# A decay scan that silences its neighbour rows through a byte table of its own, in a linear-attention and expert kernel

## The chip, the cores and the metric

One Trainium2 chip, one core. The metric is device time in microseconds (us) for one execution. PE is the matrix engine (PEld its weight loads), DVE the vector engine, ACT the scalar engine, POOL the GpSimd engine, SP the engine whose queue issues most DMAs. SBUF is the working memory and PSUM the accumulator memory that PE writes.

## The reference

Two parts follow each other. The first is a linear attention with a decaying state, over 4 batches, 8 heads, 768 tokens and a head size of 48:

```
for t in range(S):
    cur = einsum('bhd,bhe->bhde', u * k[t], v[t])
    y[:, :, t] = einsum('bhd,bhde->bhe', r[t], state + cur)
    state = w[t][..., None] * state + einsum('bhd,bhe->bhde', k[t], v[t])
```

The second takes `y` as 3072 tokens of 384 numbers. A token with `x @ w_skip > 0` goes to the best of 8 experts by `x @ w_gate`; its row becomes `x + gate * (relu(x @ w1[e]) @ w2[e])`. The other rows stay as they are.

## The kernel before

**Attention.** The tokens are cut into 24 chunks of 128 (6 for each batch). A chunk's decays `w`, reads `r` and keys `k` lie in one SBUF tile `wrk` (three of them take turns): partitions hold head halves and channels, the free axis holds 4 head pairs of 130 columns for `w` (128 decays and two zeros, with a head column in front), and 4 times 128 for `r` and `k`. Only partitions 16 to 111 are the chunk's own rows. The load brings all 128, so that the 32 outer ones are rows of neighbouring chunks; `rowsk` is a column that holds 1 on the chunk's own partitions and 0 on the others.

Two scans on DVE turn the decays into products. `prep_scan` (L274) runs backwards, `state = max(state * w, table)`, where the byte table `ones_at`, kept in the PSUM tile `pss`, holds a 1 at the end of each head pair, so that the products start anew there. The result `q` is each position's product to the end of the chunk. `prep_keys` takes the reciprocal of the whole product (L290) and puts it at the four head columns of `w`. `prep_reads` (L299) scans forwards over these heads and decays and gives `rh`, the factor of the reads. For all chunks but the first, the reciprocal goes to `hd`, four words of `pss`, and a multiplication by `rowsk` (L292) carries it to the head columns: neighbours' heads become 0, and so do their rows of `rh`.

POOL multiplies: `rk = r*k` (L283), `kq = k*q` (L294), `rp = r*rh` (L304). PE then works through a fixed order in each round: `update` (L359), `outputs` (L378 and L382 into `psY`), `scores` of the next chunk (L326 into `psA`), a transpose (L316), `bonus_sums` (L345 into `psY`) and `rows_out` (L394). Between scores and outputs, DVE masks the scores (L332, twice) and scales the bonus in place in `psY` (L349); L378 adds to `psY` and so waits for L349. ACT evicts `psY` (L387, `xT`), and L345 of the next chunk waits for that.

**Router.** After each 6 chunks a generator `router` is dripped into the following rounds: small DVE operations (L412 to L464, most with results in `pss`), a few matmuls into `pss` (ranks, L435 to L440; places, L511), and the rows `hot` of 256 columns, which ACT makes, but for some by DVE in `one_hot` (L470). For the last two chunks of the third group, `one_hot` compares with `iotap`, a copy of the counting row in `pss`; for the last group with `iota` in SBUF.

**Experts.** From about 156 us on PE runs the 8 experts with weights split in two parts.

In attention the order on each engine is the order in which the code is written: in round `s` the calls are `update(s)`, `carry(s)`, `prep_scan(s+2)`, router pieces, `outputs(s)`, `prep_keys(s+2)`, `prep_reads(s+2)`, `evict(s)`, `scores(s+1)`, `mask(s+1)`, `bonus(s+1)`. Waits between engines are placed by a framework that follows tiles: a write to one part of `pss` is ordered behind other engines' work on `pss`, too.

Of the kernel before, what the change touches and what calls it, by code (L numbers as in the profile page):

```python
# [8 lines left out]
F32 = mybir.dt.float32  # L9
BF16 = mybir.dt.bfloat16  # L10
F32R = mybir.dt.float32r
I32 = mybir.dt.int32
U32 = mybir.dt.uint32
U8 = mybir.dt.uint8
AF = mybir.ActivationFunctionType
ALU = mybir.AluOpType
# [5 lines left out]
P = 128  # L22
# [5 lines left out]
NP = H // 2  # L28
# [3 lines left out]
CW = P + 2  # L32
# [24 lines left out]
def rwkv_moe_kernel(ctx, tc, wrk, wrk0, vN, uP, wgs, wgp, w12, cst, out):  # L57
    nc = tc.nc
# [63 lines left out]
    with tc.tile_pool(name="att", bufs=2) as att, \  # L122
# [52 lines left out]
        rowsk = keep.tile([P, 1], F32, name="rowsk")  # L175
        ident = c_sb[:, C_ID:C_ID + P]
        tri = c_sb[:, C_TRI:C_TRI + P]
        iota = keep.tile([P, 2 * P], BF16, name="iota")
# [26 lines left out]
        def scratch(words):  # L205
            at = [next(at_) for _ in range(words)][0]
            return pss[:, at:at + words]

        ones_w = scratch(NP * CW // 4 + 1)
        ones_at = ones_w.bitcast(U8)  # L210
        hd = scratch(NP).rearrange("p (a o) -> p a o", o=1)
        iotaw = scratch(P)
        iotap = iotaw.bitcast(BF16)
        small3 = {nm: scratch(NC * w).rearrange("p (c e) -> p c e", c=NC)
                  for nm, w in (("lg", E + 1), ("dl", E), ("km", 1), ("sm", 1))}

        def clear_w(eng, i):
            eng.memset(wrk_sb[i][:, :R_OFF], 1.0)
# [4 lines left out]
        def setup():  # L223
            clear_w(nc.gpsimd, 0)
            nc.gpsimd.memset(vt_sb[0], 0.0)
            clear_rk(nc.vector, 0)
            load_chunk(0)
            nc.vector.memset(warm, 0.0)
            nc.gpsimd.memset(vt_sb[1], 0.0)
            load_chunk(1)  # L230
            load_v(0)
            nc.vector.memset(pss, 0.0)
            ints = ones_w.bitcast(U32)
            for a in range(NP):
                at = (a + 1) * CW - 1
                nc.vector.memset(ints[:, at // 4:at // 4 + 1], 1 << 8 * (at % 4))
            nc.vector.tensor_reduce(rowsk, ident[:, KO:LO], axis=AX, op=ALU.add)
            nc.scalar.activation(junk0, warm[:, 0:1], AF.Exp)
            for z in psa:
                nc.scalar.copy(z.rearrange("p a j -> p (a j)"), warm)  # L240
            nc.gpsimd.memset(vt_sb[2], 0.0)
            nc.scalar.copy(ubk_sb, u_sb.rearrange("p (a o) -> p a o", o=1).to_broadcast([P, NP, D]))
            for g in range(2):
                nc.tensor.matmul(psy2[:, g].rearrange("p s j -> p (s j)"), warm[:, :P], warm,
                                 start=True, stop=True, skip_group_check=True)
            nc.tensor.matmul(psu.rearrange("p a j -> p (a j)"), warm[:, :P], warm[:, :NP * HP],
                             start=True, stop=True, skip_group_check=True)
# [38 lines left out]
        def prep_keys(i):  # L286
            wk = work[i]
            heads = wk["w"][:, 0:NP * CW].rearrange("p (a j) -> p a j", a=NP)
            at = heads[:, :, 0:1]
            nc.vector.reciprocal(hd if i > 0 else at, wk["q"][:, :, 0:1])  # L290
            if i > 0:
                nc.vector.tensor_scalar(at, hd, rowsk, None, op0=ALU.mult)  # L292
            kq = wk["kq"] = att.tile([P, NP, P], F32, tag="kq", name=f"kq{i}")
            nc.gpsimd.tensor_tensor(kq, wk["k"], wk["q"][:, :, 1:1 + P], op=ALU.mult)  # L294

        def prep_reads(i):
            wk = work[i]
            rh = wk["rh"] = att.tile([P, NP, CW], F32, tag="rh", name=f"rh{i}", bufs=2)
            nc.vector.tensor_tensor_scan(  # L299
                rh.rearrange("p a j -> p (a j)"), wk["w"][:, 0:NP * CW], ones_at[:, :NP * CW],  # L300
                1.0, op0=ALU.mult, op1=ALU.max)
            rp = wk["rp"] = att.tile([P, NP, P], F32, tag="rp", name=f"rp{i}", bufs=3)
            eng = nc.gpsimd if i > 0 else nc.vector
            eng.tensor_tensor(rp, wk["r"], rh[:, :, :P], op=ALU.mult)  # L304
# [101 lines left out]
        def router(i0, m):  # L406
# [17 lines left out]
                                           op0=ALU.is_gt, op1=ALU.mult)  # L424
# [38 lines left out]
            r1 = rall[:, i0:i0 + m]  # L463
# [3 lines left out]

            def one_hot(c):
                hot = att.tile([P, 2 * P], BF16, tag="hot", name=f"hot{i0}_{c}", bufs=NC)
                nc.vector.tensor_scalar(hot, iota if last else iotap, r1[:, c], None,  # L470
                                        op0=ALU.is_equal)
                hots[c] = hot

# [7 lines left out]
            last = i0 + m == n  # L481
# [104 lines left out]

        with tc.manual_schedule():
            setup()
            fill(FILL0)
            for s in range(-2, n + 1):  # L590
                on = lambda i: 0 <= i < n
                if s + 4 < n:
                    load_chunk(s + 4)
                if on(s + 3) and s + 3 >= 1:
                    load_v(s + 3)
                if s == -2:
                    to = wgp_sb.rearrange("p (s g) x -> p g s x", g=2)
                    nc.sync.dma_start(to[:, 0, :, :2 * D], wgp[:, :2, :2 * D])
                    for o in range(2):
                        nc.sync.dma_start(to[half(o), 1, :, :2 * D], wgp[half(1 - o), :2, :2 * D])  # L600
                        for g in range(2):
                            at = 2 * (g ^ o)
                            nc.sync.dma_start(to[half(o), g, :, 2 * D:],
                                              wgp[half(g), at:at + 2, 2 * D:])
                if s == 1:
                    nc.sync.dma_start(c_sb[:, C_IOTA:], cst[:, C_IOTA:])
                if s == LATE:
                    nc.sync.dma_start(wgs_sb, wgs)
                if on(s - 1):
                    store(s - 1)  # L610
                for i0, m in GROUPS:
                    if i0 + m == s:
                        pace[0] = 1 if i0 + m < LATE else 2
                        later.append(router(i0, m))
                        if i0 + m == LATE:
                            later.append(early())
                if on(s):
                    update(s)
                    carry(s)
                if on(s + 2):  # L620
                    prep_scan(s + 2)
                drip(pace[0])
                if on(s):
                    outputs(s)
                flush()
                if on(s + 2):
                    prep_keys(s + 2)
                    drip(pace[0])
                    if s != -1:
                        prep_reads(s + 2)  # L630
                if s == -2:
                    bonus_keys(0)
                    nc.gpsimd.memset(vt_sb[3], 0.0)
                    nc.gpsimd.memset(onesb, 1.0)
                    nc.gpsimd.memset(ohs, 0.0)
                    nc.gpsimd.memset(key, 0.5)
                if on(s):
                    evict(s)
                if on(s + 1):
                    scores(s + 1)  # L640
                    rows_of_keys(s + 1)
                    drip(2 * pace[0])
                    mask(s + 1, 0)
                    mask(s + 1, 1)
                    drip(pace[0])
                    bonus_sums(s + 1)
                    bonus(s + 1)
                if s == -1:
                    prep_reads(1)
                if on(s + 2):  # L650
                    prep_check(s + 2)
                for _ in range(min(2, len(marks))):
                    marks.popleft()()
                if s == n - 1:
                    early_tokens(0)
                if on(s):
                    rows_out(s)
                flush()
                if s in (1, 2, 3):
                    nc.scalar.copy(*((trib, tri), (identb, ident),  # L660
                                     (iota, c_sb[:, C_IOTA:C_IOTA + 2 * P]))[s - 1])
                if s == 4:
                    nc.scalar.copy(iotaw, iota.bitcast(F32))
                k = s + 1 - W_AT
                for eq, k0 in (((0, 1), 0), ((1, 0), 9), ((0, 0), 16), ((1, 1), 18)):
                    if k == k0:
                        gens[eq] = load_weights(*eq)
                    if k0 <= k < k0 + 3:
                        next(gens[eq])
                if 3 <= k < 9:  # L670
                    split_slice(0, 3 + k, nc.gpsimd)
                if 12 <= k < 18:
                    split_slice(1, k - 12, nc.gpsimd)
# [349 lines left out]
```

## Time and profile before

| | |
|---|---|
| time, median of 3 (lowest to highest) | 302.96 us (302.51 to 303.55) |
| the profiled execution's own time | 301.18 us |
| its span in the trace | 299.4 us |
| PE busy | 275.0 us (92%) |
| DVE busy | 223.8 us (75%) |
| ACT busy | 168.1 us (56%) |
| POOL busy | 138.6 us (46%) |

The span is from the first to the last instruction in the trace; 1.78 us of the profiled time lie outside it. Shares are means over attention (about 10 to 156 us) and experts (from there to the end), which have different limits. Times in rows are us from the span's start.

### The profile page before, as it was taken

How to read it: one execution, taken by the hardware profiler on the slowest of the kernel's cores; microseconds unless marked ns; L12 is line 12 of the kernel's file. 1: busy time of each engine (PE TensorE's matmuls, PEld its weight loads, DVE VectorE, ACT ScalarE, POOL GpSimd, SP SyncE). 2: the span in 40 equal slices, each digit the busy share in tenths (PEclk: the TensorE clock that was granted, in tenths of full speed). 3: DMA queues.
4: the chain of work that ended last, by engine and by line, in shares of the span. 5: the costliest groups of instructions: out<-in, count | busy, mean ns of one | idle time of the engine just before them, and what ended most of it. 6: DMA issues, size and time to landing. Idle time of an engine off the chain costs nothing.

```text
span 299.4 us, 8963 instructions
## 1 busy us (share of the span) xinstructions
PE 275.0 (92%) x3581; PEld 247.8 (83%) x3581; DVE 223.8 (75%) x434; ACT 168.1 (56%) x470; POOL 138.6 (46%) x136
## 2 busy tenths in 40 slices
PE   6697998998889979879999999999999999999993
PEld 2476877777767867768798999999999999999993
DVE  7869999898989988986373788784958859496320
ACT  3265645779565986587432485581837649183310
POOL 4867765969975689776115761402011020201101
PEclk9999999999999999999999999999999999999999
DMA  7979999996799968865604798866265663620001
GB/s 217 246 198 311 349 352 371 309 303 194 240 332 297 333 187 285 219 210 180 209 28 114 231 373 308 274 207 234 71 231 208 210 251 129 237 107 26 9 2 41
DMA packets 26548, 64.62 MB, mean 216 GB/s; under 512 B 4886, under 2 KB 15930, under 8 KB 26496
## 3 DMA queue, kind: packets, MB, share of 16 engines
q1 hardware_dynamic: 23904, 58.14, 59.4%
q0 software_dynamic: 2048, 5.48, 5.5%
q8 instruction: 30, 0.49, 0.7%
q10 hardware_dynamic: 544, 0.33, 0.6%
q14 instruction: 22, 0.18, 0.2%
HBM read 56.88 MB, written 7.86 MB: 216 GB/s over the span
## 4 chain that ended last, share of the span: by engine, by line
issue 32%; PE 12%; DVE 7%; DMA 7%; POOL 6%; ACT 5%; POOLq 1%; SPq 0%; DVEq 0%
POOL out L745 5%; DMA r<-w 4%; PE psY L378 2%; PE psH L115 2%; PE psA L326 2%; PE psX L394 2%; DMA vt<-wrk 2%; PE psY L382 1%; DMA xg<-out,idr 1%; PE psY L345 1%; DVE w2l L90 1%; DVE psY L349 1%; DVE asb L332 1%; ACT xT L387 1%; PE psT L316 1%
## 5 line engine op out<-in xcount | busy, mean ns | idle before, releaser
L745 POOL DMA_INDIRECT out<-fin,ids x16 | 16.9, 1058 | 101.1 <-DVE fin L840 93.3
L814 ACT ACTIVATE hh<-psH 128x256 fp32r<-128x256 f32 x60 | 23.1, 384 | 55.2 <-PE psH L809 52.1
L809 PE MATMUL psH<-xTh,w1l 128*128 128x256 f32 x168 | 47.5, 283 | 0.0
L808 PE MATMUL psH<-xTl,w1h 128*128 128x256 f32 x168 | 47.5, 283 | 0.0
L807 PE MATMUL psH<-xTh,w1h 128*128 128x256 f32 x168 | 47.5, 283 | 0.0
L831 PE MATMUL psO<-w2h,hh 128*128 128x384 f32 x120 | 40.9, 341 | 0.0
L833 PE MATMUL psO<-w2h,hl 128*128 128x384 f32 x120 | 40.2, 335 | 0.0
L832 PE MATMUL psO<-w2l,hh 128*128 128x384 f32 x120 | 40.1, 334 | 0.0
L819 DVE SCALAR_TENSOR_TENSOR hl<-psH,hh 128x256 fp32r<-128x256 f32 x60 | 25.2, 420 | 12.3 <-ACT hh L814 12.0
L378 PE MATMUL psY<-asb,v 128*48 128x128 f32 x384 | 26.5, 276 | 8.4 <-DVE psY L349 8.4
L304 POOL TENSOR_TENSOR rp<-wrk,rh 128x512 f32<-128x512 f32 x23 | 27.2, 1182 | 12.5 <-DVE rh L299 7.6
L283 POOL TENSOR_TENSOR rk<-wrk 128x512 f32<-128x512 f32 x24 | 31.3, 1304 | 3.6 <-DMA wrk<-wrk 3.6
L332 DVE TENSOR_TENSOR asb<-psA,c_sb 128x512 f32<-128x512 f32 x48 | 30.5, 677 | 3.0 <-PE psA L326 2.8
L274 DVE TENSOR_TENSOR_SCAN q<-wrk,pss 128x520 f32<-128x520 f32 x24 | 29.3, 1222 | 4.5 <-DMA wrk<-wrk 4.4
L294 POOL TENSOR_TENSOR kq<-wrk,q 128x512 f32<-128x512 f32 x24 | 28.3, 1180 | 8.6 <-DVE q L274 4.7
L809 PEld LDWEIGHTS psH<-xTh,w1l 128*128 128x128 f32 x168 | 32.2, 192 | 0.0
L808 PEld LDWEIGHTS psH<-xTl,w1h 128*128 128x128 f32 x168 | 32.2, 192 | 0.0
L807 PEld LDWEIGHTS psH<-xTh,w1h 128*128 128x128 f32 x168 | 32.2, 191 | 0.0
L299 DVE TENSOR_TENSOR_SCAN rh<-wrk,pss 128x520 f32<-128x520 f32 x24 | 29.7, 1236 | 1.7
L89 ACT CAST w2h<-r 128x512 fp32r<-128x512 f32 x48 | 27.9, 625 | 2.0 <-DMA r<-w 2.0
L90 DVE TENSOR_TENSOR w2l<-r,w2h 128x512 fp32r<-128x512 f32 x42 | 27.8, 687 | 1.5 <-ACT w2h L89 0.5
L378 PEld LDWEIGHTS psY<-asb,v 128*48 128x48 f32 x384 | 20.4, 123 | 10.0 <-DVE psY L349 9.8
(149 smaller groups left out, 594.3 us busy)
## 6 DMA issues: line engine op xcount, KB each, us to landing
r<-w SPq DMA_DIRECT2D x48, 512.0 KB, 5.3
wrk<-wrk SPq DMA_DIRECT2D x22, 772.5 KB, 5.8
v<-vN SPq DMA_DIRECT2D x24, 192.0 KB, 5.2
out<-x SPq DMA_DIRECT2D x24, 192.0 KB, 4.6
vt<-wrk SPq DMA_DIRECT2D x46, 96.0 KB, 5.3
wrk<-wrk SPq DMA_DIRECT2D x1, 579.4 KB, 4.8
wrk<-wrk SPq DMA_DIRECT2D x1, 384.0 KB, 4.4
out<-fin,ids POOLq DMA_INDIRECT x16, 3.9
```

The costliest lines, as they stand in the source:

```text
L90: (eng or nc.vector).tensor_tensor(dst_l, src, dst_h.bitcast(F32), op=ALU.subtract)
L283: nc.gpsimd.tensor_tensor(work[i]["rk"].rearrange("p a j -> p (a j)"), t[:, R_OFF:K_OFF], t[:, K_OFF:V_OFF], op=ALU.mult)
L299: nc.vector.tensor_tensor_scan(rh.rearrange("p a j -> p (a j)"), wk["w"][:, 0:NP * CW], ones_at[:, :NP * CW], 1.0, op0=ALU.mult, op1=ALU.max)
L332: nc.vector.tensor_tensor(s, psa[g], tri.rearrange("p (o j) -> p o j", o=1).to_broadcast([P, NP, P]), op=ALU.mult)
L378: nc.tensor.matmul(y_at(a, g), v[:, 2 * a + g], wk["asb"][g][:, a], start=False, stop=True, skip_group_check=True)
L745: sc = nc.gpsimd.indirect_dma_start(out=out, out_offset=bass.IndirectOffsetOnAxis(ap=ids[:, s % 2, s // 2:s // 2 + 1], axis=0), in_=o, in_ ...
L807: nc.tensor.matmul(ps, w1h[:, o:o + P], xTh[:, kc], start=(kc == 0), stop=False)
L808: nc.tensor.matmul(ps, w1h[:, o:o + P], xTl[:, kc], start=False, stop=False)
L809: nc.tensor.matmul(ps, w1l[:, o:o + P], xTh[:, kc], start=False, stop=(kc == KC - 1))
L831: nc.tensor.matmul(pso, h[j, fc][0], w2h[:, o], start=(fc == 0), stop=False)
L832: nc.tensor.matmul(pso, h[j, fc][0], w2l[:, o], start=False, stop=False)
L833: nc.tensor.matmul(pso, h[j, fc][1], w2h[:, o], start=False, stop=(fc == FC - 1))
```

## The change

The second scan gets a byte table `reads_at` of its own, made once in `setup` by multiplying `ones_at` (seen as 32-bit words) with `rowsk`, and its start value becomes the column `rowsk` in place of the number 1. On a neighbour's rows it starts with 0 and never finds a 1, so that they come out 0 whatever stands at the heads. The reciprocal then writes the head columns directly for every chunk, and the multiplication goes. `hd` and the copy `iotap` make room in `pss`; `one_hot` always reads `iota` in SBUF, and ACT's copy to `iotap` goes.

```diff
-        hd = scratch(NP).rearrange("p (a o) -> p a o", o=1)
-        iotaw = scratch(P)
-        iotap = iotaw.bitcast(BF16)
+        reads_w = scratch(NP * CW // 4 + 1)
+        reads_at = reads_w.bitcast(U8)
...
             nc.vector.tensor_reduce(rowsk, ident[:, KO:LO], axis=AX, op=ALU.add)
+            nc.vector.tensor_scalar(reads_w.bitcast(U32), ints, rowsk, None, op0=ALU.mult)
...
-            at = heads[:, :, 0:1]
-            nc.vector.reciprocal(hd if i > 0 else at, wk["q"][:, :, 0:1])
-            if i > 0:
-                nc.vector.tensor_scalar(at, hd, rowsk, None, op0=ALU.mult)
+            nc.vector.reciprocal(heads[:, :, 0:1], wk["q"][:, :, 0:1])
...
             nc.vector.tensor_tensor_scan(
-                rh.rearrange("p a j -> p (a j)"), wk["w"][:, 0:NP * CW], ones_at[:, :NP * CW],
-                1.0, op0=ALU.mult, op1=ALU.max)
+                rh.rearrange("p a j -> p (a j)"), wk["w"][:, 0:NP * CW], reads_at[:, :NP * CW],
+                rowsk, op0=ALU.mult, op1=ALU.max)
...
-                nc.vector.tensor_scalar(hot, iota if last else iotap, r1[:, c], None,
+                nc.vector.tensor_scalar(hot, iota, r1[:, c], None,
...
-                if s == 4:
-                    nc.scalar.copy(iotaw, iota.bitcast(F32))
```

The change moves the source lines by a few: L290 becomes L289, L299 becomes L296, L332 L329, L349 L346, L447 L444, L501 L498, L520 L517. The orders of PE, POOL and SP stay the same, row for row; ACT's loses one row. On DVE 23 multiplications go and one operation comes in `setup`.

DVE in an ordinary round, before (`q` is the first scan's result, `rh` the second's, `asb` the masked scores; the wait names in brackets are the engines or DMA queues waited for):

```order
L274 SCALAR_TENSOR_TENSOR q_452<-wrk_87,pss 128x520 [waits DMAHW3_49,Pool_49]
L290 RECIPROCAL pss<-q_452 128x4 [waits DVE_49]
L292 TENSOR_SCALAR wrk_87<-pss,rowsk 128x4 [waits DVE_49]
L299 SCALAR_TENSOR_TENSOR rh_476<-wrk_87,pss 128x520 [waits DVE_49,Pool_49]
L332 TENSOR_TENSOR asb_3_505<-psA_111,c_sb 128x512 [waits PE_49]
```

and with the change:

```order
L274 SCALAR_TENSOR_TENSOR q_450<-wrk_87,pss 128x520 [waits DMAHW3_49,Pool_49]
L289 RECIPROCAL wrk_87<-q_450 128x4 [waits DVE_49]
L296 SCALAR_TENSOR_TENSOR rh_473<-wrk_87,rowsk,pss 128x520 [waits DVE_49,Pool_49]
L329 TENSOR_TENSOR asb_3_502<-psA_111,c_sb 128x512 [waits PE_49]
L329 TENSOR_TENSOR asb_3_504<-psA_112,c_sb 128x512 [waits PE_49]
```

One row is gone, and the scan has the column `rowsk` as a further operand.

DVE in a round with ranks, where PE has just written them to `pss` (`ex` are the router's exponentials, `oh` its choice), before:

```order
L274 SCALAR_TENSOR_TENSOR q_922<-wrk_86,pss 128x520 [waits DMAHW6_49,Activation_49,Pool_49]
L432 TENSOR_TENSOR oh_926<-key,pss 128x48
L290 RECIPROCAL pss<-q_922 128x4 [waits DVE_49,PE_49]
L292 TENSOR_SCALAR wrk_86<-pss,rowsk 128x4 [waits DVE_49]
L447 TENSOR_REDUCE pss<-ex_840 128x6 [waits DVE_49]
L299 SCALAR_TENSOR_TENSOR rh_956<-wrk_86,pss 128x520 [waits DVE_49,Pool_49]
```

and with the change:

```order
L274 SCALAR_TENSOR_TENSOR q_914<-wrk_86,pss 128x520 [waits DMAHW6_49,Activation_49,Pool_49]
L429 TENSOR_TENSOR oh_918<-key,pss 128x48
L289 RECIPROCAL wrk_86<-q_914 128x4 [waits DVE_49]
L444 TENSOR_REDUCE pss<-ex_832 128x6 [waits DVE_49,PE_49]
L296 SCALAR_TENSOR_TENSOR rh_947<-wrk_86,rowsk,pss 128x520 [waits DVE_49,Pool_49]
```

The wait for PE has moved from the reciprocal, which no longer writes `pss`, to the sum behind it.

DVE in a round with places, before (`sg` is what PE multiplies for them, `os` a sum of the choices):

```order
L501 TENSOR_TENSOR sg_1341<-oh_926,vals_987 128x240
L290 RECIPROCAL pss<-q_1337 128x4 [waits DVE_49,PE_49]
L292 TENSOR_SCALAR wrk_87<-pss,rowsk 128x4 [waits DVE_49]
L520 TENSOR_REDUCE os_1375<-oh_926 128x8
L299 SCALAR_TENSOR_TENSOR rh_1378<-wrk_87,pss 128x520 [waits DVE_49,Pool_49]
```

and with the change:

```order
L274 SCALAR_TENSOR_TENSOR q_1325<-wrk_87,pss 128x520 [waits DMAHW3_49,Pool_49]
L498 TENSOR_TENSOR sg_1329<-oh_918,vals_978 128x240
L289 RECIPROCAL wrk_87<-q_1325 128x4 [waits DVE_49]
L517 TENSOR_REDUCE os_1362<-oh_918 128x8
L296 SCALAR_TENSOR_TENSOR rh_1365<-wrk_87,rowsk,pss 128x520 [waits DVE_49,PE_49,Pool_49]
```

Here the wait for PE has moved to the scan itself, behind the reciprocal and the small sum.

## Rows read from the trace of the kernel before

**Rows 1.** Waits of PE, longest in total: us, times, longest.

```profile
PE psY L378 <- DVE psY L349: 8.4, 10, 1.8
```

**Rows 2.** Timeline of PE: start, us, instruction; in brackets idle before and releaser.

```profile
26.34 1.08 PE L378 MATMUL psY<-asb,v 128*48 128x128 f32 x16 [1.80 <-DVE psY L349]
...
36.62 0.30 PE L378 MATMUL psY<-asb,v 128*48 128x128 f32 x1
...
52.39 1.08 PE L378 MATMUL psY<-asb,v 128*48 128x128 f32 x16 [1.01 <-DVE psY L349]
...
58.76 1.08 PE L378 MATMUL psY<-asb,v 128*48 128x128 f32 x16 [0.59 <-DVE psY L349]
...
122.97 1.08 PE L378 MATMUL psY<-asb,v 128*48 128x128 f32 x16 [0.90 <-DVE psY L349]
...
133.01 0.65 PE L345 MATMUL psY<-rk,ubk_sb 64*48 64x128 f32 x16 [0.97 <-ACT xT L387]
```

**Rows 3.** Timeline of DVE in an ordinary round.

```profile
31.19 1.23 DVE L274 TENSOR_TENSOR_SCAN q<-wrk,pss 128x520 f32<-128x520 f32 x1
32.45 0.19 DVE L290 RECIPROCAL pss<-q 128x4 f32<-128x4 f32 x1
32.67 0.22 DVE L292 TENSOR_SCALAR wrk<-pss,rowsk 128x4 f32<-128x4 f32 x1
33.01 1.24 DVE L299 TENSOR_TENSOR_SCAN rh<-wrk,pss 128x520 f32<-128x520 f32 x1
...
35.95 1.23 DVE L274 TENSOR_TENSOR_SCAN q<-wrk,pss 128x520 f32<-128x520 f32 x1
```

**Rows 4.** Timeline of DVE: chunk 0, which has no multiplication, and chunk 3's first scan.

```profile
5.36 0.18 DVE L290 RECIPROCAL wrk<-q 128x4 f32<-128x4 f32 x1
5.57 1.24 DVE L299 TENSOR_TENSOR_SCAN rh<-wrk,pss 128x520 f32<-128x520 f32 x1
...
21.45 1.24 DVE L274 TENSOR_TENSOR_SCAN q<-wrk,pss 128x520 f32<-128x520 f32 x1 [2.72 <-DMA wrk<-wrk]
```

**Rows 5.** Timeline of DVE in a round with the router's first operations.

```profile
47.79 0.21 DVE L415 TENSOR_REDUCE mx<-pss 128x6 f32<-128x48 f32 x1
...
48.52 0.22 DVE L418 TENSOR_TENSOR pss<-pss,mx 128x48 f32<-128x48 f32 x1
48.84 1.24 DVE L299 TENSOR_TENSOR_SCAN rh<-wrk,pss 128x520 f32<-128x520 f32 x1
```

**Rows 6.** Timeline of DVE in a round with ranks.

```profile
54.35 0.19 DVE L290 RECIPROCAL pss<-q 128x4 f32<-128x4 f32 x1 [0.79 <-PE pss L440]
...
54.84 0.21 DVE L447 TENSOR_REDUCE pss<-ex 128x6 f32<-128x48 f32 x1
55.15 1.24 DVE L299 TENSOR_TENSOR_SCAN rh<-wrk,pss 128x520 f32<-128x520 f32 x1
```

**Rows 7.** Timeline of DVE in a round with places.

```profile
77.83 0.19 DVE L290 RECIPROCAL pss<-q 128x4 f32<-128x4 f32 x1 [0.55 <-PE pss L511]
...
78.38 1.24 DVE L299 TENSOR_TENSOR_SCAN rh<-wrk,pss 128x520 f32<-128x520 f32 x1
```

**Rows 8.** Timeline of DVE in the third router group's first operations.

```profile
118.68 0.19 DVE L290 RECIPROCAL pss<-q 128x4 f32<-128x4 f32 x1 [0.28 <-ACT ex L420]
...
119.04 0.20 DVE L423 SCALAR_TENSOR_TENSOR dsk<-pss,c_sb 128x48 f32<-128x48 f32 x1
```

**Rows 9.** Instruction groups of DVE by form: count, busy us, mean ns, idle before.

```profile
L449 DVE TENSOR_SCALAR pss<-pss 128x6 f32<-128x6 f32 x4 | 0.7, 172 | 0.1
```

**Rows 10.** Timeline of POOL in the round of rows 3.

```profile
32.50 1.18 POOL L294 TENSOR_TENSOR kq<-wrk,q 128x512 f32<-128x512 f32 x1 [0.50 <-DVE q L274]
```

**Rows 11.** Timeline of DVE and POOL around two of the four `sg`.

```profile
75.75 1.27 POOL L90 TENSOR_TENSOR w2l<-r,w2h 128x512 fp32r<-128x512 f32 x1 [0.22 <-ACT lgs L401]
...
75.89 1.39 DVE L501 TENSOR_TENSOR sg<-oh,vals 128x240 bf16<-128x240 bf16 x1
...
135.54 0.38 DVE L501 TENSOR_TENSOR sg<-oh,vals 128x240 bf16<-128x240 bf16 x1
```

## The prediction

> **What bounds the kernel now.** I began with the waits of PE, since the experts are PE's alone and can only follow when attention ends. The longest wait in attention is L378's for the bonus scaled by DVE: 8.4 us in 10 places [rows 1]. The timeline of PE says where they are [rows 2]. Between the places PE runs without a gap: from 26.34 to 36.62 there are two ordinary rounds, 5.14 us each. DVE needs 4.76 us for the same round, from `q` at 31.19 to `q` at 35.95 [rows 3]. So in an ordinary round PE is the limit, and DVE time saved there is worth nothing. DVE is the limit only where it carries router operations as well, or where a DMA made it late (the scan at 21.45 waited 2.72 us for its chunk [rows 4]). There, what DVE saves on the way to L349 reaches the end, up to the length of PE's wait.
>
> **The change, part by part.**
>
> *The multiplication.* In an ordinary round the reciprocal starts at 32.45, L292 at 32.67 and the second scan at 33.01: 0.56 us from reciprocal to scan [rows 3]. Chunk 0 has no multiplication, and there the scan follows after 0.21 [rows 4], 0.03 more than the reciprocal lasts. Behind L292, which lasts 0.22, the scan follows 0.34 after its start, 0.12 more than it lasts. Of that, 0.03 is the same hand-over, and I put the other 0.09 down to the second wait that later chunks' scans have (POOL beside DVE), which stays. So the scan comes 0.56 - 0.21 - 0.09 = 0.26 earlier. The bounds are 0.22 (L292's length alone) and 0.35 (no second wait).
>
> *Where a router operation shares the place*, more goes, because the reciprocal no longer writes `pss` and leaves the chain of operations that do:
> - Router start: from L415 at 47.79 to the scan at 48.84 it is 1.05 us, with reciprocal, multiplication and L418 in between [rows 5]. With the change L418 needs only L415's result (some 0.28 with the reciprocal issued in between), and the scan follows L418 by 0.32 as now: 0.45 saved.
> - Ranks: the reciprocal waits for PE until 54.35, the scan starts at 55.15 [rows 6]. Now L447 waits instead and can start at 54.35; the scan follows it by 0.31: 0.49 saved. The reciprocal falls into the 0.79 of waiting.
> - Places: the reciprocal waits until 77.83, the scan starts at 78.38 [rows 7]. Now the scan itself waits, with one wait more on its list, for which I take 0.07: 0.48 saved.
> - The third group starts in another order: reciprocal at 118.68, behind a wait for ACT, then L292, then L423 at 119.04 [rows 8]. L423 then waits for ACT in their place: 0.36 saved.
>
> *The column as start value.* No scan with a column as start value is in the trace. L292, a small operation with such a column, lasts 0.22 us [rows 3]; L449, one with a number in its place, 0.17 [rows 9]. The difference, 0.05, is my value for each scan. Below I take nothing, above all of L292's 0.22.
>
> *The rest.* The new operation in `setup` and everything else ahead of 21.45 cost nothing: the scan there waits 2.72 us for a DMA that they don't issue [rows 4]. ACT's copy of 128 words goes from an engine that isn't the limit in that round. `hot` from SBUF may run faster, or wait for POOL; at worst for one POOL multiplication, 1.18 us [rows 10]. It comes ahead of L345 at 133.01, where PE waits 0.97 us for ACT in any case [rows 2]; with what the reciprocal saves in the same round, about 0.3, that covers it, and so I cost it at nothing. For the same reason the saving in that round is worth nothing. Without this cover the worst case is 1.18 - 0.3 = 0.9 us. The DMA and POOL queues keep their orders; their transfers are asked for as their buffers come free, a little earlier.
>
> **The sum.** Of the 10 places where L378 waits for L349, six lie behind saved work, four of them shown [rows 2]:
> - 26.34, behind the DMA: one multiplication, 0.26.
> - 52.39: a multiplication and a router start, 0.26 + 0.45 = 0.71, of 1.01 waited.
> - 58.76: ranks, 0.49, of 0.59.
> - The second group repeats these two, but begins with places: 0.48 + 0.45 = 0.93, and ranks 0.49.
> - 122.97, third group: places and its start, 0.48 + 0.36 = 0.84, of 0.90.
>
> The other four give nothing: one lies ahead of 21.45, two are behind scores that PE itself has just made, one is the round ahead of 133.01. The sum is 0.26 + 0.71 + 0.49 + 0.93 + 0.49 + 0.84 = 3.72. Nine scans lie on these chains, 9 x 0.05 = 0.45. That leaves **3.27 us**. Between the groups ACT, with `hot`, sets PE's pace, but its run of work starts from PE's transposes, so what was gained is passed on. The experts start by as much sooner. The profiled execution took 301.18 us, its span 299.4 and 1.78 around it: 301.18 - 3.27 = 297.9. It ran 1.78 us below the median of 302.96, so on the median I predict 302.96 - 3.27 = **299.7 us**. With the column's cost at its bounds, the gain is 3.72 or 3.72 - 9 x 0.22 = 1.74 us: 299.2 to 301.2.
>
> **Rivals.**
>
> *The scan now excludes POOL (slower).* In rows, an `sg`, which reads two SBUF tensors, lasts 0.38 us at 135.54 but 1.39 at 75.89, where it ends (77.28) just after a POOL operation that began 0.14 before it (77.02) [rows 11]. The second scan so far reads one operand from SBUF, `wrk`; its table is in PSUM. Now `rowsk`, in SBUF, is read too. If that makes it wait as `sg` did, it waits in each round for `kq`, which `q` releases as well: from 32.50 to 33.68 [rows 10]. It would start 0.67 later than now. An ordinary round of DVE becomes 4.76 + 0.67 = 5.43 against PE's 5.14, 0.29 longer, some 14 times; in the nine places of the sum 0.67 is lost each time: 4.1 + 6.0 = 10 us, **313 us**. It decides against the change as soon as the scan's delay passes the 0.26 saved. Against it: L292 reads `rowsk` from SBUF beside POOL's work and lasts 0.22 [rows 3], but its other operand lies in PSUM. The Trainium skill (SBUF — State Buffer, § Who interferes with whom) states such a rule: a Vector instruction with two SBUF inputs and a GpSimd instruction that reads SBUF keep each other out for a whole instruction. By that rule, if a column counts as an input, the time would be this rival's 313 us, otherwise the sum's; the trace agrees with it for two tensors (0.38 and 1.39 us), and for a column no run here shows it. I give this rival 7 in 100.
>
> *The reciprocal waits for POOL (no change).* It now goes from SBUF to SBUF while POOL works. The one row of that form lasts 0.18 [rows 4]. In an ordinary round it starts 0.05 ahead of `kq` and would come first; in router rounds it would meet POOL in the middle of an operation of 1.18. Nine places at a mean of some 0.35 lost give about 3.2 us, all of the gain: **302.9 us**. 8 in 100.
>
> *The gain stops at the next wait.* L345 at 133.01 waits for ACT behind work that POOL delays; there, saved DVE time is lost. If the ACT-paced stretches behind the first two groups are also fed by something other than PE, only the third group's 0.84 - 0.10 = 0.74 remains: **302.2 us**. The rows of ACT there follow each other from a transpose of PE on, which speaks against it. 15 in 100.
>
> *A costly start value.* If the column costs each scan 0.22 or more without any exclusion, 1.7 us or less is left: **301.2 us** and above. 8 in 100, half of it still faster.
>
> **How the numbers follow.** 62 in 100 for the forecast, by its bounds 299.2 to 301.2; 0.3%, 0.9 us, is about what a measurement of this kernel can tell from no change. Faster: 62, half of the stopped gain (8) and 4 of the costly start value, 74. No change: 8, 7 and 3, in all 17 after taking 1 of the reciprocal's to the other side. Slower: 7, that 1, and 1 of the costly value, 9. The range takes in the forecast's bounds, half a us below for the spread of the runs shown, and above the stopped gain and part of the reciprocal's case: 298.7 to 302.5. The exclusion at 313 and half of "no change" stay outside, with the tail below.
>
> **What would show it.** In the profile after: no multiplication in 23 chunks; reciprocal to scan 0.30 in ordinary rounds, not 0.56; the second scan at 1.24 to 1.30 (at 1.9 or more, or with a start at the end of `kq`, the exclusion is there); L378's wait for L349 down from 8.4 to about 5 us; waits at 52.39, 58.76 and 122.97 shorter by about 0.6, 0.4 and 0.7; L345's waits for ACT longer by no more than a few tenths; the experts starting some 3 us sooner. The prediction is wrong if the scan lengthens by more than 0.2, if the reciprocal lasts over 0.3, or if PE's waits for ACT grow by what those for DVE lose.

## The result, and the profile after

After the change the kernel takes 299.5 us (median of 17 runs, 298.21 to 301.45). The kernel before, on the same chip, took 302.9 (17 runs, 301.33 to 304.16). The ratio is 0.9896, 95% interval 0.9878 to 0.9915: by it 3.15 us faster, by the interval 2.6 to 3.7. The prediction said 299.7 and 3.27. Medians here and below are over all runs, ratios over those in the faster of two states that executions of this kernel fall into.

The profiled execution after has a span of 297.9 us, only 1.5 below the 299.4 of before. The waits of PE by kind (total us, times, longest us) show L378's old wait, now in L375, at 4.8 us instead of 8.4 [rows 1], and ACT as the next in line. The last row is ACT's from before:

```profile
PE psY L375 <- DVE psY L346: 4.8, 9, 1.1
PE psY L342 <- ACT xT L384: 2.8, 4, 0.9
```

```profile
PE psY L345 <- ACT xT L387: 3.5, 5, 1.0
```

The timeline of PE after shows where (start, us, instruction; in brackets idle before and releaser). The rows from 53.38 on answer to [rows 2]; the first two are ahead of them:

```profile
12.52 0.64 PE L356 MATMUL psu<-v,kt 128*64 128x48 f32 x16 [2.06 <-DMA v<-vN]
16.46 1.97 PE L323 MATMUL psA<-rp,kq 64*64 64x128 f32 x32 [1.29 <-POOL rp L301]
...
42.84 1.08 PE L375 MATMUL psY<-asb,v 128*48 128x128 f32 x16 [0.41 <-DVE psY L346]
53.38 1.08 PE L375 MATMUL psY<-asb,v 128*48 128x128 f32 x16 [0.43 <-DVE psY L346]
59.33 1.08 PE L375 MATMUL psY<-asb,v 128*48 128x128 f32 x16 [0.17 <-DVE psY L346]
...
87.34 1.08 PE L375 MATMUL psY<-asb,v 128*48 128x128 f32 x16 [0.42 <-DVE psY L346]
93.30 1.08 PE L375 MATMUL psY<-asb,v 128*48 128x128 f32 x16 [0.17 <-DVE psY L346]
...
121.54 1.08 PE L375 MATMUL psY<-asb,v 128*48 128x128 f32 x16 [0.86 <-DVE psY L346]
127.99 1.08 PE L375 MATMUL psY<-asb,v 128*48 128x128 f32 x16 [1.07 <-DVE psY L346]
131.57 0.65 PE L342 MATMUL psY<-rk,ubk_sb 64*48 64x128 f32 x16 [0.46 <-ACT xT L384]
...
150.14 0.18 PE L432 MATMUL pss<-oh,trib 128*128 128x48 bf16 x1 [0.38 <-DVE oh L429]
```

Rows of before that [rows 2] doesn't have:

```profile
41.22 1.08 PE L378 MATMUL psY<-asb,v 128*48 128x128 f32 x16 [0.41 <-DVE psY L349]
...
87.65 1.08 PE L378 MATMUL psY<-asb,v 128*48 128x128 f32 x16 [1.25 <-DVE psY L349]
...
94.03 1.08 PE L378 MATMUL psY<-asb,v 128*48 128x128 f32 x16 [0.59 <-DVE psY L349]
...
121.17 0.18 PE L435 MATMUL pss<-oh,trib 128*128 128x48 bf16 x1 [0.27 <-DVE oh L432]
...
128.92 1.08 PE L378 MATMUL psY<-asb,v 128*48 128x128 f32 x16 [0.57 <-DVE psY L349]
...
151.58 0.18 PE L435 MATMUL pss<-oh,trib 128*128 128x48 bf16 x1 [0.38 <-DVE oh L432]
```

This execution began badly, for a reason outside the change. PE waited 2.06 us for a load of `v`, then ran for some us at half its clock (last section), and came to the bonus wait at 42.84, where before it was there at 41.22. The same load was waited for 0.64 us in the first kernel below, whose first chunks are those of after, and 2.12 us in the kernel before with a column. So spans can't be compared directly. From here on I use **the stretch**: from this bonus wait, which all these kernels share, to the matmul of the last group's ranks (L435 before, L432 after), which opens the part that nothing here touches. Windows of PE, first of before, then of after (from:to, length, busy time, instructions, granted clock as a share of 2.4 GHz, busy share of the DMA engines, GB/s):

```profile
41.22:151.58 110.36, 98.92 (x1959) 1.00 0.82 262
```

```profile
42.84:150.14 107.30, 98.61 (x1959) 1.00 0.83 265
```

Same work, same clock, 3.06 us less, 2.75 of it time in which PE stood idle (11.44 before, 8.69 after). From there to the end both need the same (147.8 us).

Between these waits as anchors the 3.06 splits up. The spacing before is compared with the spacing after:

| from the anchor of before, to | before, us | after, us | gained | sum said, less 0.05 a scan |
|---|---|---|---|---|
| 41.22 to 52.39 (router start) | 11.17 | 10.54 | 0.63 | 0.61 |
| to 58.76 (ranks) | 6.37 | 5.95 | 0.42 | 0.44 |
| to 87.65 (places, router start) | 28.89 | 28.01 | 0.88 | 0.83 |
| to 94.03 (ranks) | 6.38 | 5.96 | 0.42 | 0.44 |
| to 122.97 (third group) | 28.94 | 28.24 | 0.70 | 0.74 |
| to 128.92 (`hot`) | 5.95 | 6.45 | -0.50 | 0 |
| to 133.01 (L345 waits for ACT) | 4.09 | 3.58 | 0.51 | 0 |
| to 151.58 | 18.57 | 18.57 | 0 | 0 |

On DVE the timeline after shows the four places that answer to [rows 3], [rows 5], [rows 6] and [rows 7], and the row of the third group that answers to [rows 8]:

```profile
28.43 0.18 DVE L289 RECIPROCAL wrk<-q 128x4 f32<-128x4 f32 x1
28.71 1.30 DVE L296 TENSOR_TENSOR_SCAN rh<-wrk,rowsk,pss 128x520 f32<-128x520 f32 x1
...
49.20 0.21 DVE L412 TENSOR_REDUCE mx<-pss 128x6 f32<-128x48 f32 x1
...
49.77 1.30 DVE L296 TENSOR_TENSOR_SCAN rh<-wrk,rowsk,pss 128x520 f32<-128x520 f32 x1
...
55.34 0.21 DVE L444 TENSOR_REDUCE pss<-ex 128x6 f32<-128x48 f32 x1 [0.67 <-PE pss L437]
55.66 1.30 DVE L296 TENSOR_TENSOR_SCAN rh<-wrk,rowsk,pss 128x520 f32<-128x520 f32 x1
...
78.43 1.30 DVE L296 TENSOR_TENSOR_SCAN rh<-wrk,rowsk,pss 128x520 f32<-128x520 f32 x1 [0.38 <-PE pss L508]
...
117.54 0.21 DVE L420 SCALAR_TENSOR_TENSOR dsk<-pss,c_sb 128x48 f32<-128x48 f32 x1 [0.23 <-ACT ex L417]
...
124.72 1.41 DVE L467 TENSOR_SCALAR hot<-iota,rall 128x256 bf16<-128x256 bf16 x2
```

From the reciprocal to the scan it is 0.28 us (0.56 before). Router start: from L412 to the scan 0.57 (1.05 before). Ranks: from the end of the wait to the scan 0.32 (0.80 before). Places: the scan itself starts as the wait ends (0.55 after it before). The last row holds two of the `hot` comparisons; one of them took 1217 ns, as the POOL multiplication of 1.19 us that began at 124.67 ran beside it.

Groups of DVE's instructions by form (count, busy us, mean ns, idle before) give the scan's price: 1296 ns, before 1236 for the same 24.

```profile
L296 DVE TENSOR_TENSOR_SCAN rh<-wrk,rowsk,pss 128x520 f32<-128x520 f32 x24 | 31.1, 1296 | 3.7 <-PE pss L508 1.9
L289 DVE RECIPROCAL wrk<-q 128x4 f32<-128x4 f32 x24 | 4.3, 178 | 0.4
```

### The profile page after: what moved, and what is told of

It reads as the page before. It is cut to its first block, busy times and chain, and to the rows that moved or that the text cites. A ratio compares the mean times of both kernels' runs of the same rounds, so it can differ in the third digit from the quotient of the medians.

```text
span 297.9 us, 8938 instructions
## 1 busy us (share of the span) xinstructions
PE 277.1 (93%) x3581; PEld 249.5 (84%) x3581; DVE 220.3 (74%) x412; ACT 167.1 (56%) x469; POOL 138.8 (47%) x136
## 4 chain that ended last, share of the span: by engine, by line
issue 33%; PE 20%; ACT 9%; DVE 8%; POOL 6%; DMA 5%; POOLq 1%; SPq 0%; DVEq 0%
POOL out L740 5%; DMA vt<-wrk 3%; PE psY L375 3%; PE psA L323 3%; PE psX L391 2%; PE psH L115 2%; ACT psu L365 1%; ACT dd L474 1%; PE psY L379 1%; ACT hot L475 1%; DVE psY L346 1%; DMA v<-vN 1%; PE psT L313 1%; ACT xT L384 1%; PE psY L342 1%
## 5 line engine op out<-in xcount | busy, mean ns | idle before, releaser
L329 DVE TENSOR_TENSOR asb<-psA,c_sb 128x512 f32<-128x512 f32 x48 | 30.6, 679 | 5.8 <-PE psA L323 5.8
L296 DVE TENSOR_TENSOR_SCAN rh<-wrk,rowsk,pss 128x520 f32<-128x520 f32 x24 | 31.1, 1296 | 3.7 <-PE pss L508 1.9
L375 PE MATMUL psY<-asb,v 128*48 128x128 f32 x384 | 26.7, 276 | 4.8 <-DVE psY L346 4.8
L835 DVE SCALAR_TENSOR_TENSOR fin<-psO,gates,xg 128x384 f32<-128x384 f32 x15 | 9.3, 618 | 25.7 <-PE psO L828 25.7
```

The lines of the kernel that those rows point to most:

```text
L296: nc.vector.tensor_tensor_scan(rh.rearrange("p a j -> p (a j)"), wk["w"][:, 0:NP * CW], reads_at[:, :NP * CW], rowsk, op0=ALU.mult, op1=AL ...
L329: nc.vector.tensor_tensor(s, psa[g], tri.rearrange("p (o j) -> p o j", o=1).to_broadcast([P, NP, P]), op=ALU.mult)
L375: nc.tensor.matmul(y_at(a, g), v[:, 2 * a + g], wk["asb"][g][:, a], start=False, stop=True, skip_group_check=True)
```

## Experiments

My theory is the prediction's: the gain arises only where PE waits for DVE behind router work, each place by its own term, less the column's price; `hot` costs nothing because ACT's wait covers it. The rivals are that it arises in ordinary rounds as well, that only the multiplication's length counts, and that the column or the one-hot comparison costs something in the end. The stretch of each kernel is from its profile; times are set against the kernel before on the same chip. The four kernels of the first set had before at 304.12 us (35 runs), those of the second at 301.95 (11 runs).

**The multiplication back in nine chunks.** The changed kernel, with the multiplication (and its stop in `pss`) put back where the sum counts a place:

```diff
+BACK = (3, 7, 8, 9, 13, 14, 15, 19, 20)
...
+        hd = scratch(NP).rearrange("p (a o) -> p a o", o=1)
...
-            nc.vector.reciprocal(heads[:, :, 0:1], wk["q"][:, :, 0:1])
+            at = heads[:, :, 0:1]
+            nc.vector.reciprocal(hd if i in BACK else at, wk["q"][:, :, 0:1])
+            if i in BACK:
+                nc.vector.tensor_scalar(at, hd, rowsk, None, op0=ALU.mult)
```

> The changed kernel with the multiplication by rowsk (and the reciprocal into pss) back for the nine chunks that the sum counted: 3, 7, 8, 9, 13, 14, 15, 19, 20. The table of its own and the column as start value stay for all chunks. My theory: the gain comes from these nine alone, so it goes, and the column's 9 x 0.06 us is left as a loss: 303.2 to 303.5 us against 302.9, ratio 1.001 to 1.002; L378's wait for the bonus is back at 8.4 us or more. Rival (each of the 23 multiplications is worth the same): 14 of 23 of 3.2 us stay, 301.0 us, ratio 0.9935.

Measured: 304.44 us, ratio 1.0018 (0.9977 to 1.0059). The interval leaves out the rival's 0.9935. The stretch is 41.28 to 152.24 = 110.96 us, 0.60 more than before. L378's old waits at the first group's places are back and longer by 0.17 and 0.06 (52.57 and 59.01 answer to [rows 2]):

```profile
41.28 1.08 PE L380 MATMUL psY<-asb,v 128*48 128x128 f32 x16 [0.41 <-DVE psY L351]
...
52.57 1.08 PE L380 MATMUL psY<-asb,v 128*48 128x128 f32 x16 [1.18 <-DVE psY L351]
59.01 1.08 PE L380 MATMUL psY<-asb,v 128*48 128x128 f32 x16 [0.65 <-DVE psY L351]
...
152.24 0.18 PE L437 MATMUL pss<-oh,trib 128*128 128x48 bf16 x1 [0.38 <-DVE oh L434]
```

So fourteen chunks without the multiplication give nothing: the whole gain is in nine.

**The multiplication back in the other fourteen.** The same edit with the complementary list.

> The changed kernel with the multiplication back for the other fourteen chunks. My theory: these lie in rounds that PE paces, or ahead of a wait that hides them, so that the time stays at that of the changed kernel: 299.5 to 299.8 us, ratio 0.989 to 0.990. Rival (each multiplication is worth the same): 14 of 23 of the gain go, 301.7 us, ratio 0.996.

Measured: 301.25 us, ratio 0.9923 (0.9883 to 0.9964). The interval just takes in the rival's 0.996, so that the time alone doesn't decide; the stretch does. It is 40.75 to 148.23 = 107.48 us, 2.88 less than before and 0.18 more than after the change, where the rival would lose 14 of 23 of 3.06, 1.86 us:

```profile
40.75 1.08 PE L380 MATMUL psY<-asb,v 128*48 128x128 f32 x16 [0.41 <-DVE psY L351]
...
148.23 0.18 PE L437 MATMUL pss<-oh,trib 128*128 128x48 bf16 x1 [0.38 <-DVE oh L434]
```

The waits at the router places are those of after to 0.02 us (0.44, 0.17, 0.42, 0.17, 0.87). Of the 0.18, 0.13 lie at `hot`: the bonus wait there is 1.44 us (after: 1.07) and comes 0.36 later, and what follows gives only 0.23 of it back, as PE's wait for ACT behind it (0.46 after) is gone. Nine removals of 23 carry the gain.

**The multiplication back in four chunks only**, `BACK = (9, 13, 15, 19)`: the ranks and the places, where the reciprocal carried the wait for PE.

> The change, but with the multiplication and its chain back in the four chunks whose wait for PE the change moves (ranks in 9 and 15, places in 13 and 19). The stretch is PE's time from the bonus product near 42 us to the first weighted sum near 150 us: 110.36 us before, 107.30 after. Theory (the sum's terms stand as worked out, each place by itself): 0.49 + 0.48 + 0.49 + 0.48 = 1.94 us less a quarter us or so for the column, which stays, so the stretch is 109.1 to 109.3 us, the waits in front of the ranks' bonus are back at 0.59 or 0.65, and the reciprocal to scan in chunk 9 is 0.80. Rival (what counts is only the length of the multiplication, wherever it stands): 4 x 0.26 = 1.04 lost, a stretch of 108.3 us, and the ranks' wait is near 0.4.

Measured once: 299.81 us. The stretch, PE in it by the same columns as above, is 109.25 us:

```profile
40.95:150.20 109.25, 98.96 (x1959) 1.00 0.83 263
```

So 1.95 us are lost against after; the terms said 1.94, the rival 1.04. The ranks' wait is 0.65 at 57.93, as in the kernel with nine. What counts is the length of the chain, with the operations that it held up through `pss`, and not the 0.22 us of the instruction. The span is 297.9 us, the same as after the change, with 1.95 us less saved: PE ran at full clock at the start of this execution, a warning against reading single spans.

The same run settles the first place, which the profile of after couldn't show. In chunk 3 the multiplication is gone here. Of DVE the scan that waits for the load, of PE the matmul that waits behind it:

```profile
21.38 1.24 DVE L276 TENSOR_TENSOR_SCAN q<-wrk,pss 128x520 f32<-128x520 f32 x1 [2.58 <-DMA wrk<-wrk]
```

```profile
26.07 1.08 PE L380 MATMUL psY<-asb,v 128*48 128x128 f32 x16 [1.53 <-DVE psY L351]
```

From the one to the other it takes 4.69 us; before 26.34 - 21.45 = 4.89 [rows 2, 4]. That is 0.20 saved, against 0.26 - 0.05 = 0.21. From there to the start of the stretch all three kernels need the same 14.88 us (26.34 to 41.22 before, 26.07 to 40.95 here, 25.87 to 40.75 with the other fourteen back), so it is passed on whole.

**A column as start value, and nothing else of the change.** The kernel before, whose scan starts from an SBUF column of ones:

```diff
+        onecol = keep.tile([P, 1], F32, name="onecol")
...
+            nc.vector.memset(onecol, 1.0)
...
-                1.0, op0=ALU.mult, op1=ALU.max)
+                onecol, op0=ALU.mult, op1=ALU.max)
```

> The kernel before with one thing added: the second scan takes its start value 1 from a column in SBUF and not from the instruction. My theory: each second scan lasts 1.30 and not 1.24 us, and 9 to 10 of them count: 0.5 us slower, 303.4 us, ratio 1.0018. Rival (the scan's length comes from the new table or the zero rows, not from the column): 1.24 us and no change. Second rival (all 24 count): 1.4 us slower, 304.3, ratio 1.0047.

Measured: 305.08 us, ratio 1.0023 (0.9983 to 1.0062). The interval takes in both rivals, no change and 1.0047, so that rows must decide. The stretch is 43.42 to 154.41 = 110.99 us, 0.63 more than before, where all 24 scans would have cost 1.44. The group of DVE's scans shows the price, 60 ns each:

```profile
L301 DVE TENSOR_TENSOR_SCAN rh<-wrk,onecol,pss 128x520 f32<-128x520 f32 x24 | 31.1, 1296 | 1.7
```

It is the same with another column in another kernel, and no scan waits for POOL.

**The scan without the column.** The changed kernel, whose scan begins one element earlier: `w` moves by one column, the element ahead of it is zero, the table has a 1 (on own rows) for it, and the start value is a number.

```diff
-R_OFF = 1 + NP * CW
+W_OFF = 2
+R_OFF = W_OFF + NP * CW
...
-                rh.rearrange("p a j -> p (a j)"), wk["w"][:, 0:NP * CW], reads_at[:, :NP * CW],
-                rowsk, op0=ALU.mult, op1=ALU.max)
+                rhw[:, 1:], wk["w"][:, 0:1 + NP * CW], reads_at[:, :1 + NP * CW],
+                0.0, op0=ALU.mult, op1=ALU.max)
...
```

> The change without its price: the scan starts one element earlier, on a column of zeros and a table entry that is 1 times the row's flag, so its start value is the number 0.0 again and no column is read. Theory (the 60 ns are the column's): the scan lasts 1.24 us for 521 elements instead of 1.30, and PE's stretch from the bonus product near 42 us to the first weighted sum near 150 us shortens from 107.30 by the column's share, eight or nine scans by 0.06, to about 106.8; against the kernel before 0.988, that is 3.7 us. Rival (the 60 ns come from the table or from what else has moved, not from the column): the scan stays at 1.29 to 1.31, the stretch at 107.3 and the ratio at 0.990.

Measured: 298.93 us, ratio 0.9908 (0.9888 to 0.9928). The scan is back at 1239 ns for 521 elements. The stretch is 41.37 to 148.41 = 107.04 us: 0.26 less than after, about half of what I expected. PE's timeline shows where the rest was lost; the two rows of L329 belong to the rounds ahead of the first group's two places, the others to the second group:

```profile
47.55 1.39 PE L329 MATMUL psA<-rp,kq 64*64 64x128 f32 x32
...
54.97 0.21 PE L329 MATMUL psA<-rp,kq 64*64 64x64 f32 x1 [0.23 <-issue]
...
85.71 1.08 PE L381 MATMUL psY<-asb,v 128*48 128x128 f32 x16 [0.30 <-DVE psY L352]
...
91.60 1.08 PE L381 MATMUL psY<-asb,v 128*48 128x128 f32 x16
```

The waits for the bonus at the first group's two places, 0.43 and 0.17 after the change, are gone. Ahead of the first, PE's score matmuls took 1.39 us (after: 1.09), which the wait still hid: the place comes after 10.42 us (after: 10.54), the full 0.12 of two scans earlier. Ahead of the second they stopped for 0.23, and this place comes after 6.06 us instead of 5.95, later by 0.11 and not earlier by 0.06. At the second group's same places there is no such stop, and 0.15 and 0.07 are gained (27.86 and 5.89 us instead of 28.01 and 5.96), as expected. So 0.17 of the 0.22 that are missing from eight scans by 0.06 is one stop in one execution. Its cause is open: the profile names no wait for it. By the ratios, 0.9908 and 0.9896 on different chips, this version can't be told from the change; the profile alone puts it 0.26 us ahead.

**`hot` from PSUM again.** The changed kernel, with the counting row copied to PSUM as before (in another tile's bank) for the two late comparisons:

```diff
-                nc.vector.tensor_scalar(hot, iota, r1[:, c], None,
+                nc.vector.tensor_scalar(hot, iota if last else iotap, r1[:, c], None,
...
+                if s == 4:
+                    nc.scalar.copy(iotaw, iota.bitcast(F32))
```

> The changed kernel, but with the two hot rows of the third group read from a copy of the counting row in PSUM (in the unused half of the bank of psu), as before. My theory: the first hot row no longer takes 1.2 us, the wait of L378 at 128 us falls by some 0.9, and L345's wait for ACT behind it grows by as much, so that the time stays: ratio 0.988 to 0.991, 299.5 us. Rival (what hot loses reaches the end): 0.5 to 1 us less, 298.5 to 299.0, ratio 0.986.

Measured: 300.64 us, ratio 0.9906 (0.9866 to 0.9947), which leaves out the rival's 0.986; the stretch is 44.63 to 152.10 = 107.47, after 107.30. The two comparisons take 346 ns each and the bonus wait is short, but the next one, for ACT, has grown by as much (after: 1.07 and 0.46, in the rows at 127.99 and 131.57 above):

```profile
129.13 1.08 PE L378 MATMUL psY<-asb,v 128*48 128x128 f32 x16 [0.37 <-DVE psY L349]
133.43 0.65 PE L345 MATMUL psY<-rk,ubk_sb 64*48 64x128 f32 x16 [1.17 <-ACT xT L387]
```

The cover holds: 0.70 us move from one wait to the other.

**The multiplication from SBUF to SBUF.** The kernel before, with `hd` moved:

```diff
-        hd = scratch(NP).rearrange("p (a o) -> p a o", o=1)
+        hd = pers.tile([P, NP, 1], F32, name="hd")
```

> The kernel before, with only the place of the reciprocal's result changed from PSUM to SBUF, so that the multiplication goes from SBUF to SBUF as the one-hot comparison does after the change. Theory A (a tensor_scalar from SBUF to SBUF waits for POOL, as the comparison of 1217 ns did): the multiplication, ready just after POOL's product of the keys starts at 32.50, waits for its end, lasts 0.9 to 1.3 us in most of 23 chunks, each round of DVE grows by some 0.9 us over its 4.76 and passes PE's 5.14, and the span is 10 to 16 us longer than the 299.4 before. Rival B (the one long comparison was chance, or needs 256 bf16 columns): the multiplication lasts 0.17 to 0.25 us everywhere, and the span is within 1.5 us of before. The reciprocal, from SBUF to SBUF here too, lasts under 0.2 us by either.

Measured once: 306.91 us, 5.0 above the kernel before on this chip; span 305.1, 5.7 longer than in the profile before. The multiplication's mean is 805 ns, before 0.22 us [rows 3]; the reciprocal's stays at 176. In an ordinary round, POOL's `kq` and DVE's multiplication:

```profile
32.99 1.18 POOL L294 TENSOR_TENSOR kq<-wrk,q 128x512 f32<-128x512 f32 x1 [0.51 <-DVE q L274]
```

```profile
33.16 1.04 DVE L292 TENSOR_SCALAR wrk<-hd,rowsk 128x4 f32<-128x4 f32 x1
```

It ends at 34.20, just behind `kq` at 34.17, and the round grows from 5.14 to 5.56 us (L378 at 31.82 and 37.38). So a `tensor_scalar` of four elements waits for POOL's whole instruction when it reads and writes SBUF, and not when it reads PSUM. The mechanism was as expected; of 10 to 16 us in the span only 5.7 came. The round grew as said; why fewer rounds counted I didn't follow up.

**The table in SBUF.** The changed kernel, with only its byte table moved, so that the scan reads two SBUF tensors:

```diff
-        reads_w = scratch(NP * CW // 4 + 1)
+        reads_w = pers.tile([P, NP * CW // 4 + 1], F32, name="reads_w")
```

> The change, with only the byte table moved from PSUM to SBUF, so that the scan has two SBUF tensors. It prices the exclusion that the prediction gave 7 in 100. Theory (a second SBUF tensor makes the scan wait for POOL, while the column did not): the scan waits for POOL's product of the keys in most rounds, its mean goes from 1.30 to 1.7 us or more, the ordinary round from 5.14 to about 5.4, and the span is some 10 us longer than the 297.9 after the change (6 to 14). Rival (scans never wait for POOL, whatever they read): the scan stays at 1.29 to 1.31, and the span within 2 us of 297.9.

Measured once: 303.62 us, span 301.8, 3.9 above that after, whose bad start makes the difference too small. Scan and POOL's `kq` in an ordinary round, POOL's `rk`, and the granted clock behind the long wait for `hot`:

```profile
34.38 2.04 DVE L296 TENSOR_TENSOR_SCAN rh<-wrk,rowsk,reads_w 128x520 f32<-128x520 f32 x1
```

```profile
34.14 1.18 POOL L291 TENSOR_TENSOR kq<-wrk,q 128x512 f32<-128x512 f32 x1 [0.51 <-DVE q L274]
```

```profile
L283 POOL TENSOR_TENSOR rk<-wrk 128x512 f32<-128x512 f32 x24 | 37.5, 1564 | 1.9 <-DMA wrk<-wrk 1.9
```

```profile
130.65:135.00 4.35, 4.35 (x68) 0.64 0.72 270
```

The scan's mean is 1785 ns instead of 1296, and POOL's `rk` waits in turn, 1564 instead of 1303. A second SBUF tensor makes the scan exclude POOL; the column did not. The stretch is 110.34 us (43.53 to 153.87), 3.04 more than after. Some 1.6 us of that come from the clock at 130.65, behind a wait of 2.23 us: three groups of matmuls there take 0.95, 1.95 and 1.11 us instead of 0.65, 1.09 and 0.66. The expected 6 to 14 us was too much.

## Why the prediction was right

- **Where the gain lies.** That ordinary rounds give nothing is shown by the nine and the fourteen chunks: 0.60 us worse than before, and 2.88 us better.
- **L378's wait** fell from 8.4 to 4.8 us (about 5 was said), but that it met the figure is luck. 1.80 of the 3.6 are the wait at 26.34, which is missing after because PE itself came late there; in the run with the fourteen chunks, at full clock, 1.61 of it are left, and the sum is 6.0. And at 122.97 the wait was to shorten by about 0.7 and went only from 0.90 to 0.86. The gain of 0.70 is there all the same, ahead of it: the wait of 0.27 at 121.17 is gone, and another of 0.15, as PE comes sooner by nearly as much as DVE. What the sum needed was the length of DVE's chain, and that it had right.
- **The terms.** Over the stretch the sum says 3.27 - 0.21 = 3.06 us, and 3.06 was measured. At each of the five router places it is off by at most 0.05 (table above). The first place gives 0.20 of 0.21, seen in another run with the same chunk 3.
- **The small constants.** The multiplication's 0.26 is 0.28 by the rows, the router start's 0.45 is 0.48, the ranks' 0.49 is 0.48, the column's 0.05 is 0.06. For the places' 0.48 the rows give 0.50: from the end of PE's matmul to the scan it was 0.58 (77.80 to 78.38) and is 0.08 (78.35 to 78.43).
- **Luck in the last digits.** Without the column the sum for the stretch is 3.72 - 0.26 = 3.46; the kernel without it shows 110.36 - 107.04 = 3.32. The column's price in the stretch is 8 x 0.05 = 0.40 in the sum and 0.26 by the same two kernels. By these profiles saving and price are each 0.14 too high in the sum, and cancel. The column alone, set into the kernel before, costs 0.63. Whether the two parts don't simply add, or only the one stop of 0.23 in the kernel without the column parts them, the runs don't tell.
- **`hot`.** One of the two comparisons did wait for POOL, 1217 ns, and the round lost 0.50 us; L345's wait then fell from 0.97 to 0.46 and gave 0.51 back. The cover named in the prediction is shown from the other side by the run with PSUM, and its end by the run with the fourteen chunks, where PE no longer waits for ACT behind it and 0.13 is lost.
- **The exclusion rival** (313 us) did not occur: 24 scans last 1.29 to 1.30 us. The Trainium skill (SBUF — State Buffer, § Who interferes with whom) states the exclusion for two SBUF inputs; the run with the table in SBUF agrees (1785 ns against 1296), and for a column the runs say that it does not count. Even had it come, my price of 13 us over the forecast was too high: with the table in SBUF an ordinary round is 5.28 us (5.43 was said), and the mean over all scans is 1785 ns against 2.04 us in that round, so that in other rounds less is waited than I took. The stretch of that case was 3.04 us longer, 1.6 of it by the clock.
- **The reciprocal that waits for POOL** did not occur: 168 to 182 ns, 24 times, all from SBUF to SBUF. Some began in the middle of a POOL operation, as this one on DVE beside `kq` on POOL:

```profile
122.98 0.17 DVE L289 RECIPROCAL wrk<-q 128x4 f32<-128x4 f32 x1
```

```profile
122.87 1.18 POOL L291 TENSOR_TENSOR kq<-wrk,q 128x512 f32<-128x512 f32 x1
```

- **The gain that stops at the next wait** did not occur: L342's waits for ACT behind the groups stay (0.59, 0.82 and 0.94 us after; 0.60, 0.83 and 0.94 before), that is, ACT's work came as much sooner as PE did.
- **The costly start value** did not occur as 0.22; it costs 0.06.

## What to carry to other kernels

Before an operation is taken off an engine, list the places where the engine that sets the pace waits for it, and cost each place by the whole chain that it leaves, with the waits that move to another instruction. Here nine of 23 removals made the gain, and four of them, of 0.22 us each, were worth 0.49 because a wait for PE was no longer carried through them. And when two versions differ by a few us, compare stretches between two events that both have, since one late load at the start can hide half the gain in a single span.

## What the hardware showed that I had not expected

- **PE's clock fell behind some waits.** In the profile after, PE idled 2.06 us for `v`, and soon 0.86 and 1.29 more. Windows of PE in that profile show the granted clock at 0.50, that is 1.2 of 2.4 GHz:

```profile
16.40:18.50 2.10, 2.04 (x33) 0.50 0.20 26
18.50:20.50 2.00, 2.00 (x21) 0.50 0.88 245
```

  The matmuls of L323 at 16.46 took 1.97 us, before 1.09. Before, the same load was waited for 0.63 us, and the clock in the window from 12.00 to 16.30 stayed at 1.00. The kernel before with a column waited 2.12 us for it, and there, too, the score matmuls took 1.97. In the run with the table in SBUF it was the wait of 2.23 us (0.64 behind it); in the one with `hd` in SBUF it was 0.50 from 126.90 to 130.00, behind waits of 0.52 and 0.90 us. A single wait of 1.80 [rows 2] did not lower it. That the idle time caused it is argued from these rows, not shown by an experiment.
- **One instruction of four elements waits as long as a big one.** L292 from SBUF to SBUF lasted 1.04 us beside `kq`, for work that takes 0.22 from PSUM, while a reciprocal of the same size, from SBUF to SBUF too, took 0.17 in the middle of `kq` (122.98 above).
- **A start value in a column costs 60 ns** per scan, whichever column, and shuts nothing out.
